# Row sums of every exponential and inverse, a test of them, and a branch to a general path at the end of a fused attention and feed-forward kernel

## The chip, the cores and the metric

The kernel runs on one core of one Trainium2 chip. A core has a matrix engine (TensorE, PE in the profile, with its weight loads as PEld), a vector engine (DVE), a scalar engine for activation functions (ScalarE, ACT), a general engine (GpSimd, POOL) and a fifth one that mostly issues transfers (SyncE, SP). Each engine works through its own list of instructions in order and waits on semaphores for the others. The metric is the device time of one execution, in microseconds (us).

## The reference

Sliding-window attention over 8 batches of 8 heads, 576 positions and 64 columns a head, with a window of 64 positions, and then a gated feed-forward block over the 4608 tokens:

```python
scores = scale * np.matmul(q, k.transpose(0, 1, 3, 2))
rel = pos[:, None] - pos[None, :]
mask = (rel >= 0) & (rel < window)
scores = np.where(mask, scores, -1000000000.0)
scores = scores - np.max(scores, axis=-1, keepdims=True)
attn = np.exp(scores)
attn = attn / (np.sum(attn, axis=-1, keepdims=True) + 1e-09)
attn_out = np.matmul(attn, v)
...
x = attn_out.transpose(0, 2, 1, 3).reshape(B * S, H * D)
g = x @ w_gate
silu = g * (1.0 / (1.0 + np.exp(-g)))
val = x @ w_val
return silu * val @ w_out
```

The inputs are random numbers: q, k and v with a standard deviation of 0.1, the weights with one over the square root of their depth. All are float32, and so is the output of 4608 x 512.

## The kernel before

The tokens are worked on in NT = 9 tiles of 512. Tiles 0 to 6 and 8 hold the first 512 positions of one batch each; tile LAST = 7 holds the last 64 positions of all eight batches. The kernel never takes a row's maximum: it takes the exponential of the scaled scores as they are, masks them, sums them by a matmul with ones, and multiplies the mixed values by the inverse of that sum. The inverse is made on ScalarE as the exponential of the negative logarithm, so that both come from one table of functions.

The order of all instructions is written out by hand (manual_schedule): what is called earlier in the program stands earlier in its engine's list. A tile t goes through these stages:

- scores (L279, in tile 0 L250) writes the products of queries and keys into the two double banks two[0] and two[1]. weigh (L294, in tile 0 weigh_first, L602) takes the exponential of each into a bf16 tile eb. The vector engine masks it (L299) and adds neighbours (L304).
- This is done twice for a tile, for two halves of the heads (w = 0 and 1), into the same two double banks. The matmuls of L480 that lie in between belong to the output projection of tile t - 1 and fill TensorE's time. Markers (L387) and two small copies (fence, L776, on ScalarE, and seen, L777, on the vector engine) order the use of two other banks.
- sums (L322, in tile 0 L315) makes the row sums of the weights by matmuls with ones. log (L336) takes their logarithm, invert (L339) the exponential of the negative logarithm, in place, in the float32 tile r.
- mix (L400) multiplies the weights with the values into two[1] and two[0]; scale (L416) multiplies the result with the inverse into the bf16 tile xT.
- gate_value (L459) runs twelve groups (m = 0 to 11), each of four matmuls with the gate weights and four with the value weights. gate_end takes the silu on ScalarE (L452) and the product on the vector engine (L453) into hT. The keys and queries of tile t + 1 are transposed between the groups on the vector engine.
- The projection to the output (L480, L468) of tile t runs beside the attention of tile t + 1. For the last tile it stands alone: three row blocks by project (L468, copied to SBUF at L488 and stored at L497 and L499), and the last one by project_last (L521, copied and stored in two pieces at L525 and L526).

Two switches of ScalarE's function table happen in each tile: set_exp (L529) before the exponentials, set_silu (L532) before the gates.

After the last store, SP waits for all transfers, and all engines meet in two barriers (in the profile at L848, the line at which the program is closed). Instructions are fetched from memory by each engine's own queue (the instruction queues q8 and q14 in the profile).

Of the kernel before, what the change touches and what calls it, by code (L numbers as in the profile page):

```python
# [17 lines left out]
def kernel(  # L18
# [10 lines left out]
    nc = tc.nc  # L29
    S, D, H = 576, 64, 8  # L30
    NTOK, DFF, DM = 4608, 1536, 512
    NT = NTOK // 512
# [25 lines left out]
    identb = cst.tile([P, P], BF16, name="identb")  # L58
    ones = cst.tile([P, 512], BF16, name="ones")
    tri = cst.tile([P, 2, 64], BF16, name="tri")  # L60
    bias = cst.tile([P, 2, 4, 4, 2, 16], BF16, name="bias")
    seen = cst.tile([D, 1], FP32, name="seen")
    fence = cst.tile([D, 1], FP32, name="fence")
    past = cst.tile([P, 1], BF16, name="past")
    mask = cst.tile([P, 8, 2, 16, 4], BF16, name="mask")

    def batch(t):
        return t if t < LAST else t - 1
# [7 lines left out]
    staged, queries, weights, inverse, xT, hT = {}, {}, {}, {}, {}, {}  # L76
# [95 lines left out]
    def stage_v(t):  # L172
        new_v(t)
        load_halves(nc.sync, staged[t, "v"], t)
# [115 lines left out]
    def weigh(t, w, h, s_ps):  # L290
        n = 1024 if t == LAST else 960
        E = eb[2 * w + h]
        flat = E[:].rearrange("r s z -> r (s z)")[:, 64:64 + n]
        nc.scalar.activation(  # L294
            flat, s_ps[:].rearrange("r a b -> r (a b)")[:, 0:n], AF.Exp, scale=0.125
        )

        def masked():
            nc.vector.tensor_mul(  # L299
                flat, flat, mask[:].rearrange("r j c e y -> r (j c e y)")[:, 0:n]  # L300
            )
            both = epool.tile([P, 8, 64], BF16, name="both", tag="both")
            lo = 2 if t == LAST else 0
            nc.vector.tensor_add(both[:], E[:, 1:17:2], E[:, lo:lo + 15:2])  # L304
            weights[t, w, h] = E, both

        return masked

    def ready(masks):
        for masked in masks:  # L310
            masked()
# [21 lines left out]
        return ap.rearrange("r (e x) -> r x e", e=16)  # L333

    def log(r, d_ps):
        nc.scalar.activation(r, d_ps, AF.Ln)  # L336

    def invert(r):
        nc.scalar.activation(r, r, AF.Exp, scale=-1.0)  # L339

    def logs(t, r, d):
        if t == NT - 1:
# [43 lines left out]
    def marker(b, x):  # L386
        nc.tensor.matmul(bank[b][0:D, 0:16], ones[half(x), 0:D], ones[half(x), 0:16])  # L387
# [39 lines left out]
    def mix_half(t, w, pair):  # L427
        mix(t, w, (pair[:, 0], pair[:, 1]))
# [15 lines left out]
    def gate_tiles():  # L444
        return out_tile(), d_tile()

    def gate_end(t, m, pair):
        if m == 0:
            hT[t] = hpool.tile([P, 12, 512], BF16, name="hT", tag="hT")
        g_ps, v_ps = pair  # L450
        sg = fsb.tile([P, 512], FP32, name="sg", tag="sg")
        nc.scalar.activation(sg[:], g_ps[:], AF.Silu)  # L452
        nc.vector.tensor_mul(hT[t][:, m, :], sg[:], v_ps[:])  # L453

    def gate_value(t, m):
        pair = gate_tiles()
        for ps, w in zip(pair, (wg, wv)):
            for c in range(4):
                nc.tensor.matmul(  # L459
                    ps[:], w[:, c, P * m:P * m + P], xT[t][:, c, :],  # L460
                    start=(c == 0), stop=(c == 3),
                )
        gate_end(t, m, pair)
# [52 lines left out]
    def project_last(t, s):  # L516
        r0 = S * batch(t) + P * s
        os_ = fsb.tile([P, 512], FP32, name="os_", tag="os_", bufs=4)
        for f0, f1, o_ps in ((0, 384, bank[6]), (384, 512, bank[0])):
            for c in range(12):  # L520
                nc.tensor.matmul(  # L521
                    o_ps[:, 0:f1 - f0], hT[t][:, c, P * s:P * s + P], wo[:, c, f0:f1],
                    start=(c == 0), stop=(c == 11),
                )
            nc.vector.tensor_copy(os_[:, f0:f1], o_ps[:, 0:f1 - f0])  # L525
            nc.sync.dma_start(out[r0:r0 + P, f0:f1], os_[:, f0:f1])  # L526

    def set_exp():
        nc.scalar.preload_act_table_set("natural_log_exp_and_others")  # L529

# [9 lines left out]
    v_first = stage.tile([P, 4, H, D], FP32, name="v_f", tag="v", bufs=1)  # L540
    load_v(nc.sync, v_first, (0, 1))
    set_exp()
    nc.vector.memset(ones[:, 0:P], 1.0)
    nc.vector.memset(ones[:, P:512], 1.0)
    nc.vector.memset(joined[half(1), 0], 0.0)
# [53 lines left out]

    def weigh_first(u):  # L600
        E = eb[u][:, 1:17].rearrange("r (h y) z -> r h (y z)", h=2)
        nc.scalar.activation(E, two[u % 2][:], AF.Exp, scale=0.125)  # L602
        weights[0, u] = E

    def sums_first(u, b):
# [25 lines left out]
    lo, hi = slice(0, 2), slice(2, 4)  # L631
# [63 lines left out]
    for m in range(12):  # L695
# [21 lines left out]
        if m == 10:  # L717
            for u in range(4):
                tp = two[u % 2].bitcast(BF16)[:, u // 2, 0:512]
# [5 lines left out]
            for u in range(4):  # L725
                tp = two[u % 2].bitcast(BF16)[:, u // 2, 0:512]
# [41 lines left out]
    for t in range(1, NT):  # L768
        if t > 1:
            set_exp()  # L770
            masks = scores(t, 0)
            masks[0]()
            project_quads(t - 1, tiles, range(12), 0)
            for x in range(2):
                marker(4 + 2 * x, x)
            on_a(fence[:], bank[4][0:D, 0:1])  # L776
            on_v(seen[:], bank[6][0:D, 0:1])  # L777
            masks[1]()
            if t == 2:
                stage_v(3)  # L780
            ready(scores(t, 1))
            for x in range(2):
                marker(4 + 2 * x, x)
            project_quads(t - 1, tiles, range(7), 1)
            end = sums(t, 0, two[0:1])
            project_quads(t - 1, tiles, range(7, 12), 1)
            for w in range(2):
                mix_half(t, w, two[1 - w])
# [12 lines left out]
        on_p(past[:], xT[t][:, 3, 0:1])  # L801
        if t + 1 == LAST:
            load_last_v()
        elif t + 1 < NT and t > 1:
            cast_v(t + 1)
        if t + 2 < NT:
            load_qk(t + 2)
            if t > 1 and t + 2 != LAST:
                stage_v(t + 2)
        if t == 2:  # L810
            k_l = cast.tile([P, 4, 4, 4 * D], BF16, name="k_l", tag="c0")
        if t in (2, 3):
            load_k(k_l, [(b, S - P) for b in range(4, 8)], quarters[2 * t - 4:2 * t - 2])
        turns = (6, 7, 9, 10) if t == 1 else (1, 4, 7, 10)
        for m in range(12):
            gate_value(t, m)
            if m in turns and t + 1 < NT:
                turn(t + 1, turns.index(m))
            if (t, m) in late:
                turn_k(kT[2], k_l, late.index((t, m)))  # L820
    for s in range(3):
        project(NT - 1, s, bank[(5, 7, 4)[s]])
    project_last(NT - 1, 3)

# [1 line left out]
_INS = ['q', 'k', 'v', 'moe_w_gate', 'moe_w_val', 'moe_w_out']  # L826
# [26 lines left out]
```

## Time and profile before

| what | value |
|---|---|
| median of 3 runs | 321.78 us (321.73 to 322.04) |
| the profiled execution as a whole | 322.17 us |
| its span, first to last instruction | 320.4 us |
| granted TensorE clock, mean | 1.000 |
| ScalarE: silu of the gates, L452 | 63.9 us |
| ScalarE: exponentials of tiles 1 to 8, L294 | 29.5 us, 0.974 each |
| ScalarE: inverses, L339 | 18.6 us, 0.972 each |
| vector engine: products of the gates, L453 | 73.9 us, 0.692 each |

The span is the time from the first to the last instruction in the profile; what the execution takes beyond it (1.8 us here) lies around it. A row of the timeline gives the start in us from the span's begin, the time that the instruction or the run of equal instructions took, the engine, the line, the operation, the tile written and the one read with their shapes, the count, and in brackets the idle time of the engine just before it and what ended that. A row of the list by line gives, behind the shapes and the count, the busy time in us and the mean of one in ns. In the list of instructions of one line the durations are least, median and most, in ns.

### The profile page before, as it was taken

Reading aid. Unit: us, or ns where it says so; the run is one execution under the profiler, and the core shown is the slowest. Engines: PE = TensorE matmul, PEld = TensorE weight load, DVE = VectorE, ACT = ScalarE, POOL = GpSimd, SP = SyncE. Lnnn points to the kernel's source line nnn. Section 1 sums busy time; section 2 is a strip of 40 time slices with the busy share of each in tenths; the row PEclk is TensorE's granted clock in tenths of the full one; section 3 lists DMA queues with packets and bytes.
Section 4 is the critical chain, followed back from the end, with each engine's and each line's share of the span. In section 5 each row is a group of like instructions: output and inputs, shape, how many; then the busy total and the mean of one; then the engine's idle time right before and its main releaser. Section 6 shows DMA issues by size and latency. Waiting matters only on the chain.

```text
span 320.4 us, 8080 instructions
## 1 busy us (share of the span) xinstructions
PE 315.9 (99%) x3297; PEld 155.0 (48%) x3297; DVE 209.4 (65%) x341; ACT 170.9 (53%) x239; POOL 147.4 (46%) x268
## 2 busy tenths in 40 slices
PE   8999999999999999999999999999999999999996
PEld 4544544445444644455445544454446444544443
DVE  4855846498586846776588656866796486844422
ACT  4964666348633863377336933584347633873310
POOL 4965656867557336650861099507766300000000
PEclk9999999999999999999999999999999999999999
DMA  7999999999799549994896269719998400011003
GB/s 249 205 196 198 206 149 229 189 193 130 165 186 178 65 109 167 187 103 100 150 194 69 61 122 119 75 28 149 184 197 103 109 9 1 4 74 60 0 20 113
DMA packets 83525, 40.42 MB, mean 126 GB/s; under 512 B 64160, under 2 KB 78752, under 8 KB 83488
## 3 DMA queue, kind: packets, MB, share of 16 engines
q0 software_dynamic: 51488, 22.59, 58.7%
q1 hardware_dynamic: 31456, 16.79, 23.8%
q8 instruction: 26, 0.43, 0.5%
q10 hardware_dynamic: 544, 0.52, 0.5%
q14 instruction: 11, 0.09, 0.1%
HBM read 53.02 MB, written 9.44 MB: 195 GB/s over the span
## 4 chain that ended last, share of the span: by engine, by line
PE 97%; ACT 2%; issue 0%; DVE 0%
PE one L459 56%; PE one L468 17%; PE one L480 11%; PE two L279 3%; PE two L400 2%; PE one L435 2%; PE one L554 1%; ACT eb L602 1%; PE two L322 1%; PE one L521 1%; PE two L435 1%; PE one L322 0%; ACT r L336 0%; ACT r L339 0%; PE one L197 0%; PE two L722 0%
## 5 line engine op out<-in xcount | busy, mean ns | idle before, releaser
L452 ACT ACTIVATE sg<-one 128x512 f32<-128x512 f32 x107 | 63.9, 597 | 117.2 <-PE one L459 91.3
L453 DVE TENSOR_TENSOR hT<-sg,one 128x512 bf16<-128x512 f32 x107 | 73.9, 692 | 62.6 <-PE one L459 58.5
L459 PE MATMUL one<-xT,wg 128*128 128x512 bf16 x416 | 106.8, 379 | 0.0
L459 PE MATMUL one<-xT,wv 128*128 128x512 bf16 x416 | 106.8, 379 | 0.0
L128 POOL DMA_DIRECT2D k_s<-in_k_dram x112 | 60.4, 575 | 27.0 <-DMA q_s<-in_q_dram 13.3
L459 PEld LDWEIGHTS <-wv 128*128 128x128 bf16 x416 | 40.7, 98 | 49.1
L459 PEld LDWEIGHTS <-wg 128*128 128x128 bf16 x416 | 40.6, 98 | 48.9
L468 PE MATMUL one<-wo,hT 128*128 128x512 bf16 x252 | 56.5, 380 | 0.0
L801 POOL COPY past<-xT 128x1 bf16<-128x1 bf16 x8 | 1.5, 189 | 88.7 <-DVE xT L416 88.7
L480 PE MATMUL one<-wo,hT 64*64 64x512 bf16 x672 | 40.0, 377 | 0.0
L468 PEld LDWEIGHTS <-hT 128*128 128x128 bf16 x252 | 23.8, 98 | 29.3 <-issue 2.0
L219 DVE STREAM_TRANSPOSE kT<-k_s 128x512 bf16<-128x512 bf16 x28 | 35.9, 1283 | 0.2 <-DMA vb<-in_v_dram 0.2
L416 DVE TENSOR_TENSOR xT<-two,r 128x512 bf16<-128x512 f32 x34 | 21.2, 683 | 20.6 <-ACT r L339 16.7
L294 ACT ACTIVATE eb<-two 128x960 bf16<-128x960 f32 (+1 forms) x32 | 29.5, 974 | 3.0 <-PE two L279 2.9
L480 PEld LDWEIGHTS <-hT 64*64 64x64 bf16 x672 | 18.6, 107 | 13.8
L299 DVE TENSOR_TENSOR eb<-eb,mask 128x960 bf16<-128x960 bf16 (+1 forms) x32 | 20.9, 654 | 5.7 <-ACT eb L294 5.6
L209 DVE STREAM_TRANSPOSE qT<-q_s 128x512 bf16<-128x512 bf16 x32 | 22.2, 700 | 0.1
L339 ACT ACTIVATE r<-r 128x1024 f32<-128x1024 f32 (+1 forms) x20 | 18.6, 972 | 0.1
L304 DVE TENSOR_TENSOR both<-eb 128x512 bf16<-128x512 bf16 x32 | 13.6, 425 | 1.1
L93 POOL DMA_DIRECT2D q_s<-in_q_dram x24 | 13.0, 549 | 1.6 <-DMA v<-in_v_dram 1.0
L154 POOL DMA_DIRECT2D vb<-in_v_dram x16 | 11.0, 692 | 6.1 <-DMA wo<-in_moe_w_out_dram 3.5
L529 ACT ACT_TABLE_LOAD x9 | 11.5, 1283 | 2.0 <-issue 1.9
(137 smaller groups left out, 241.9 us busy)
## 6 DMA issues: line engine op xcount, KB each, us to landing
k_s<-in_k_dram POOLq DMA_DIRECT2D x112, 56.0 KB, 5.3
q_s<-in_q_dram POOLq DMA_DIRECT2D x24, 248.0 KB, 6.0
v_f<-in_v_dram SPq DMA_DIRECT2D x40, 128.0 KB
wg<-in_moe_w_gate_dram POOLq DMA_DIRECT2D x5, 256.0 KB, 8.4
wv<-in_moe_w_val_dram POOLq DMA_DIRECT2D x5, 256.0 KB, 8.9
q_f<-in_q_dram SPq DMA_DIRECT2D x4, 256.0 KB
wo<-in_moe_w_out_dram POOLq DMA_DIRECT2D x2, 512.0 KB, 10.7
vb<-in_v_dram POOLq DMA_DIRECT2D x16, 64.0 KB, 6.6
```

The source lines that it names most:

```text
L128: nc.gpsimd.dma_start(k_s[p0:p0 + 32, g, :, 0:w], k[b, a:H:2, s:s + P].rearrange("u (r e) d -> r u (e d)", e=4) [:, :, 32 * c:32 * c + w],)
L209: nc.vector.transpose(queries[t][:, u, :].rearrange("r (e x) -> r e x", e=16), staged[t][0][:, u].rearrange("r (e d) -> r e d", d=D)[:, :, ...
L219: nc.vector.transpose(dst[:, u, :].rearrange("r (g x e) -> r g e x", g=4, e=4), k_s[:, :, u].rearrange("r g (e d) -> r g e d", d=D)[:, :, ...
L294: nc.scalar.activation(flat, s_ps[:].rearrange("r a b -> r (a b)")[:, 0:n], AF.Exp, scale=0.125)
L299: nc.vector.tensor_mul(flat, flat, mask[:].rearrange("r j c e y -> r (j c e y)")[:, 0:n])
L339: nc.scalar.activation(r, r, AF.Exp, scale=-1.0)
L416: nc.vector.tensor_mul(x, o_ps, r)
L452: nc.scalar.activation(sg[:], g_ps[:], AF.Silu)
L453: nc.vector.tensor_mul(hT[t][:, m, :], sg[:], v_ps[:])
L459: nc.tensor.matmul(ps[:], w[:, c, P * m:P * m + P], xT[t][:, c, :], start=(c == 0), stop=(c == 3),)
L468: nc.tensor.matmul(o_ps[:], hT[t][:, c, P * s:P * s + P], wo[:, c, :], start=(c == 0), stop=(c == 11),)
L480: nc.tensor.matmul(tiles[s][half(y)], hT[t][half(x), c, r0:r0 + 64], wo[half(x), c, :], start=not back and c == 0, stop=bool(back) and c = ...
```

## The change

Four things are added.

First, each exponential of scores (L294 and L602) and each inverse (L339) also gives the sum of its results along a row, one float32 column each, in a tile spread with 6 * NT + 2 = 56 columns; extent hands out the columns. Second, the logarithm gets a bias: a column floor that holds 2 to the power of -60 is added to its argument, so that a sum of zero doesn't give an infinite logarithm. Third, survey, called in the gates of the last tile behind group m = 4, compares all 56 columns with 2 to the power of 30 on the vector engine, takes the least of each row, sums the 128 rows by a matmul with ones into one element per row of two[0], and copies it to an integer column count. Fourth, at the end of the program every engine loads count into a register, and where it is below 128 the program runs a general path over all eight batches: attention with each row's maximum, a feed-forward block and its stores, over the output that is already there. Where it is 128, the engines go through a short block that brings the semaphores to the values that the general path would have left, and jump to the end.

In the built program the order of all other instructions on each engine is as before. The general path stands between the short block and the end: 8,001 instructions of TensorE, 3,385 of the vector engine, 1,593 of GpSimd, 1,369 of ScalarE and 577 of SP.

```diff
+    spread = cst.tile([P, 6 * NT + 2], FP32, name="spread")
+    within = cst.tile([P, 2], BF16, name="within")
+    count = cst.tile([P, 1], mybir.dt.int32, name="count")
+    floor = cst.tile([P, 1], FP32, name="floor")
+    LEAST, MOST = 2.0 ** -60, 2.0 ** 30
+    columns_used = [0]
+
+    def extent():
+        columns_used[0] += 1
+        return spread[:, columns_used[0] - 1:columns_used[0]]
...
         nc.scalar.activation(
-            flat, s_ps[:].rearrange("r a b -> r (a b)")[:, 0:n], AF.Exp, scale=0.125
+            flat, s_ps[:].rearrange("r a b -> r (a b)")[:, 0:n], AF.Exp, scale=0.125,
+            accum_out=extent(),
         )
...
     def log(r, d_ps):
-        nc.scalar.activation(r, d_ps, AF.Ln)
+        nc.scalar.activation(r, d_ps, AF.Ln, bias=floor[:])
 
     def invert(r):
-        nc.scalar.activation(r, r, AF.Exp, scale=-1.0)
+        nc.scalar.activation(r, r, AF.Exp, scale=-1.0, accum_out=extent())
...
+    def survey():
+
+        used = spread[:, 0:columns_used[0]]
+        fine = fsb.tile([P, 64], FP32, name="fine", tag="fine", bufs=1)[:, 0:columns_used[0]]
+        nc.vector.tensor_single_scalar(fine, used, MOST, op=ALU.is_le)
+        nc.vector.tensor_reduce(within[:, 0:1], fine, axis=mybir.AxisListType.X, op=ALU.min)
+        nc.tensor.matmul(two[0][:, 0, 0:1], ones[:, 0:P], within[:, 0:1])
+        nc.vector.tensor_copy(count[:], two[0][:, 0, 0:1])
+
+    def general_attention(b):
+
+        x_b = v12[:].rearrange("r g i h d -> r (g i h d)")[:, 0:4 * S]
...
+        for hd in range(H):
...
+            for c, (lo, hi) in enumerate(chunks):
...
+                nc.vector.tensor_reduce(top, s, axis=mybir.AxisListType.X, op=ALU.max)
+                nc.vector.tensor_scalar(top, top, -1.0, 0.0, op0=ALU.mult, op1=ALU.add)
+                nc.scalar.activation(s, s, AF.Exp, bias=top, accum_out=total)
...
+        return x_b
+
+    def general_ffn(b, x_b):
...
+            for m in range(12):
+                for w, ps_ in ((wg, bank[4]), (wv, bank[5])):
+                    for c in range(4):
+                        nc.tensor.matmul(
+                            ps_[:, 0:n], w[:, c, P * m:P * m + P], x_b[:, c, lo:hi],
+                            start=c == 0, stop=c == 3,
+                        )
...
+                nc.sync.dma_start(out[at:at + rows], os_[0:rows])
...
     set_exp()
+    nc.vector.memset(floor[:], LEAST)
...
-        nc.scalar.activation(E, two[u % 2][:], AF.Exp, scale=0.125)
+        nc.scalar.activation(E, two[u % 2][:], AF.Exp, scale=0.125, accum_out=extent())
...
             gate_value(t, m)
+            if t == NT - 1 and m == 4:
+                survey()
...
     project_last(NT - 1, 3)
+    good = nc.values_load(count[0:1, 0:1], min_val=0, max_val=P)
+    with tc.If(good < P, preferred_fallthrough_block=False):
+        for b in range(8):
+            x_b = general_attention(b)
+            general_ffn(b, x_b)
```

More of the change, by code (lines that the diff above doesn't have):

```diff
@@ new lines, in general_attention @@
+    def general_attention(b):
+        x_b = v12[:].rearrange("r g i h d -> r (g i h d)")[:, 0:4 * S]
+        x_b = x_b.rearrange("r (c s) -> r c s", c=4)
+        chunks = [(P * c, min(S, P * c + P)) for c in range(5)]
+        set_exp()
+        for hd in range(H):
+            u, h = hd // 2, hd % 2
+            wide = {}
+            for n, (src, tag) in (("q", (q, "q")), ("k", (k, "k"))):
+                f = stage.tile([P, 5, D], FP32, name=n + "_g", tag=tag)
+                nc.sync.dma_start(f[:, 0:4], src[b, hd, 0:512].rearrange("(c r) d -> r c d", r=P))
+                nc.sync.dma_start(f[0:64, 4], src[b, hd, 512:S])
+                bf = epool.tile([P, 5, D], BF16, name=n + "_h", tag="both")
+                nc.vector.tensor_copy(bf[:, 0:4], f[:, 0:4])
+                nc.vector.tensor_copy(bf[0:64, 4], f[0:64, 4])
+                tp = bank[4 if n == "q" else 5].bitcast(BF16)
+                for c, (lo, hi) in enumerate(chunks):
+                    nc.tensor.transpose(
+                        tp[0:D, lo:hi], bf[0:hi - lo, c], identb[0:hi - lo, 0:hi - lo]
+                    )
+                wide[n] = att.tile([P, S], BF16, name=n + "_w", tag="qT")
+                nc.vector.tensor_copy(wide[n][0:D], tp[0:D, 0:S])
+            vf = stage.tile([P, 5, D], FP32, name="v_g", tag="v", bufs=1)
+            nc.sync.dma_start(vf[:, 0], v[b, hd, 0:P])
+            nc.sync.dma_start(vf[:, 1:5], v[b, hd, 64:S].rearrange("(c r) d -> r c d", r=P))
+            vh = epool.tile([P, 5, D], BF16, name="v_h", tag="both")
+            nc.vector.tensor_copy(vh[:], vf[:])
+            for c, (lo, hi) in enumerate(chunks):
+                nq, k0 = hi - lo, max(0, lo - 64)
+                nk = hi - k0
+                s_ps = bank[6][0:nq, 0:nk]
+                nc.tensor.matmul(s_ps, wide["q"][0:D, lo:hi], wide["k"][0:D, k0:hi])
+                w = fsb.tile([P, 512], FP32, name="w_g", tag="sg")
+                s = w[0:nq, 0:nk]
+                nc.scalar.activation(s, s_ps, AF.Copy, scale=0.125)
+                for sign, base in ((1, lo - k0), (-1, 63 + k0 - lo)):
+                    nc.gpsimd.affine_select(
+                        out=s, in_=s, compare_op=ALU.is_ge, fill=-1e9,
+                        base=base, pattern=[[-sign, nk]], channel_multiplier=sign,
+                    )
+                top, total = w[0:nq, 256:257], w[0:nq, 257:258]
+                nc.vector.tensor_reduce(top, s, axis=mybir.AxisListType.X, op=ALU.max)
+                nc.vector.tensor_scalar(top, top, -1.0, 0.0, op0=ALU.mult, op1=ALU.add)
+                nc.scalar.activation(s, s, AF.Exp, bias=top, accum_out=total)
+                nc.vector.tensor_scalar(total, total, 1.0, 1e-9, op0=ALU.mult, op1=ALU.add)
+                nc.vector.reciprocal(total, total)
+                e = epool.tile([P, 192], BF16, name="e_g", tag="e_g", bufs=1)
+                nc.vector.tensor_scalar(e[0:nq, 0:nk], s, total, 0.0, op0=ALU.mult, op1=ALU.add)
+                tp = bank[7].bitcast(BF16)
+                pT = fsb.tile([P, 2, P], BF16, name="p_g", tag="p_g", bufs=1)
+                parts = [(0, P)] + ([(P, nk)] if nk > P else [])
+                for i, (j0, j1) in enumerate(parts):
+                    nc.tensor.transpose(
+                        tp[0:j1 - j0, P * i:P * i + nq], e[0:nq, j0:j1], identb[0:nq, 0:nq]
+                    )
+                    nc.vector.tensor_copy(
+                        pT[0:j1 - j0, i, 0:nq], tp[0:j1 - j0, P * i:P * i + nq]
+                    )
+                o_ps = bank[4][half(h), 0:nq]
+                for i, (j0, j1) in enumerate(parts):
+                    nc.tensor.matmul(
+                        o_ps, vh[0:j1 - j0, c + i], pT[0:j1 - j0, i, 0:nq],
+                        start=i == 0, stop=i == len(parts) - 1,
+                    )
+                nc.vector.tensor_copy(x_b[half(h), u, lo:hi], o_ps)
+        return x_b
@@ new lines, in general_ffn @@
+    def general_ffn(b, x_b):
+        set_silu()
+        for lo, hi in ((0, 512), (512, S)):
+            n = hi - lo
+            h_b = hpool.tile([P, 12, 512], BF16, name="h_b", tag="hT")
+            for m in range(12):
+                for w, ps_ in ((wg, bank[4]), (wv, bank[5])):
+                    for c in range(4):
+                        nc.tensor.matmul(
+                            ps_[:, 0:n], w[:, c, P * m:P * m + P], x_b[:, c, lo:hi],
+                            start=c == 0, stop=c == 3,
+                        )
+                sg = fsb.tile([P, 512], FP32, name="sg", tag="sg")
+                nc.scalar.activation(sg[:, 0:n], bank[4][:, 0:n], AF.Silu)
+                nc.vector.tensor_mul(h_b[:, m, 0:n], sg[:, 0:n], bank[5][:, 0:n])
+            for r0 in range(0, n, P):
+                rows = min(P, n - r0)
+                for c in range(12):
+                    nc.tensor.matmul(
+                        bank[6][0:rows], h_b[:, c, r0:r0 + rows], wo[:, c, :],
+                        start=c == 0, stop=c == 11,
+                    )
+                os_ = fsb.tile([P, 512], FP32, name="os_", tag="os_", bufs=4)
+                nc.vector.tensor_copy(os_[0:rows], bank[6][0:rows])
+                at = S * b + lo + r0
+                nc.sync.dma_start(out[at:at + rows], os_[0:rows])
```

## The prediction

> **What bounds the kernel now.** I read the page's busy times first, then the chain of work that ended last, then the timeline around the lines that the diff touches.
>
> ```profile
> span 320.4 us, 8080 instructions
> ...
> PE 315.9 (99%) x3297; PEld 155.0 (48%) x3297; DVE 209.4 (65%) x341; ACT 170.9 (53%) x239; POOL 147.4 (46%) x268
> ```
>
> ```profile
> PE 97%; ACT 2%; issue 0%; DVE 0%
> ```
>
> TensorE is busy for all but 4.5 us and carries 97% of the chain; ScalarE's 2% all lie before 13.3 us. So a microsecond counts only where it makes TensorE wait, or where it stands before TensorE's first steady work or behind its last. The added work sits on ScalarE, which is 53% busy, so its sum (56 sums, 27 biases) says little; the waits between the two engines decide. Three places: the first batch, the meeting of ScalarE and TensorE in each steady stage, and the end.
>
> The first batch, ScalarE in order of time (start, length, line):
>
> ```profile
> 7.53 1.02 ACT L602 ACTIVATE eb<-two 128x1024 bf16<-128x1024 f32 x1 [0.82 <-PE two L250]
> ...
> 9.04 0.60 ACT L336 ACTIVATE r<-one 128x512 f32<-128x512 f32 x1
> 9.54 1.02 ACT L602 ACTIVATE eb<-two 128x1024 bf16<-128x1024 f32 x1
> 10.44 0.63 ACT L339 ACTIVATE r<-r 128x512 f32<-128x512 f32 x1
> 11.05 0.60 ACT L336 ACTIVATE r<-two 128x512 f32<-128x512 f32 x1
> 11.68 0.63 ACT L339 ACTIVATE r<-r 128x512 f32<-128x512 f32 x1
> 12.22 1.92 ACT L602 ACTIVATE eb<-two 128x1024 bf16<-128x1024 f32 x2
> ```
>
> No line after the first has idle time before it: ScalarE runs without a gap from 7.53 to the end of the third exponential at 13.22, and TensorE's L365 starts at 13.27. Every nanosecond added in this run is paid.
>
> A steady stage (token tile 3), ScalarE and then TensorE:
>
> ```profile
> 106.17 1.83 ACT L294 ACTIVATE eb<-two 128x960 bf16<-128x960 f32 x2
> 108.31 0.15 ACT L776 COPY fence<-one 64x1 f32<-64x1 f32 x1 [0.31 <-PE one L387]
> 108.73 1.83 ACT L294 ACTIVATE eb<-two 128x960 bf16<-128x960 f32 x2 [0.26 <-PE two L279]
> 110.53 1.02 ACT L336 ACTIVATE r<-two 128x1024 f32<-128x1024 f32 x1
> ```
>
> ```profile
> 108.07 0.62 PE L279 MATMUL two<-qT,kT 64*64 64x128 bf16 x31
> 111.39 1.01 PE L400 MATMUL two<-eb,vb 64*64 64x128 bf16 x64
> ```
>
> The second scores of a stage overwrite the two tiles that the first two exponentials read. The second exponential ends at 108.00; its first dependent matmul, the third of L279's run, starts at 108.09. A hand-over costs 0.05 (the fence copy ends at 108.47, the marker matmul behind it starts at 108.52), so this wait has 0.03 us of room. It is the tightest of the stage.
>
> **The change, part by part.** A row sum is given by 56 activations: 4 at L602, 32 at L294, 20 at L339. No row of this trace has one. Lower end: 0, the sum rides along. Upper end: a further ScalarE instruction for a 128x1 result, at an activation's fixed cost: L339 takes 0.63 us for 512 columns and 1.06 for 1024, which leaves 0.20 at none. Nearest is the fence copy, one column, 0.15 alone; neighbours overlap by 0.10 (exponentials are 0.97 long and 0.87 apart), so it adds 0.05 between others and 0.15 where something waits for it. I take d = 0.10. The bias of the 27 logs becomes a column in memory: 0 to 0.15 by the same copy, I take b = 0.08. The Trainium skill, "ScalarE: Activation LUTs", section on what ACT_TABLE_LOAD costs, states about 93 ns for each per-partition pointer operand; no run here shows it yet, and by it the sum below would be 0.1 us higher.
>
> First batch: from 7.53 to 13.22 there are five sums (three exponentials, two inverses) and two logs: 5d + 2b = 0.66 us (0 to 1.3). Behind it the other inverses have room: the gates' first matmul with the third column block starts 0.64 after that block's scaling ends.
>
> Each stage of tiles 2 to 8, seven in all. (A) L279 waits for two sums more: 2d - 0.03 = 0.17 (0 to 0.37). The fence copy has 0.31 of room behind the exponential, so it takes nothing more. (B) The second half of L400 writes the tile that the log at 110.53 reads; the log ends at 111.55 and that half starts at 111.81, 0.20 of room behind the hand-over. The log itself is held by L322's totals and could have started 0.07 earlier. So two sums and one bias cost (2d - 0.07) + b - 0.20 = 0.01 (0 to 0.28). The later logs and inverses (2b + 2d = 0.36) have over a microsecond before the gates read their blocks: nothing. Seven times 0.18 = 1.26 (0 to 4.6). Tile 1's waits have 0.20 or more of room: nothing. ScalarE in all: 1.9 us (0 to 5.9).
>
> The survey comes behind the fifth gate group (m = 4) of the last tile. Its TensorE matmul stands in the program order between that group and the next and waits for the vector engine's compare and reduce, which stand behind that group's product:
>
> ```profile
> 294.78 1.03 PE L459 MATMUL one<-xT,wg 128*128 128x512 bf16 x4
> 295.05 0.69 DVE L453 TENSOR_TENSOR hT<-sg,one 128x512 bf16<-128x512 f32 x1 [1.04 <-PE one L459]
> ```
>
> TensorE would start group 5 at 294.78. The product ends at 295.74; a compare of 128x56 at the 0.19 of L571 (128x64), a hand-over of 0.05, a reduce at 0.15 to 0.19, less up to 0.09 of overlap with the product (L416's products are 0.69 long and 0.60 apart), another hand-over: 296.1 to 296.2. The matmul takes 0.05 more. Behind it the whole gate stream is queued, nothing later is slack, so TensorE loses 1.45 us (1.2 to 1.7). The copy of the count fits into the 1.04 that the vector engine idles. The one memset at the start lies in its wait for the key load (0.7 before the cast at 4.53).
>
> The end:
>
> ```profile
> 317.37 0.81 SPq L526 DMA_DIRECT2D out_dram<-os__4647  x2
> 317.46 0.29 DVE L525 COPY os__4647<-two 128x128 f32<-128x128 f32 x1
> ```
>
> ```profile
> q8 instruction: 26, 0.43, 0.5%
> ...
> q14 instruction: 11, 0.09, 0.1%
> ```
>
> ```profile
> L848 SPq DRAIN x3: 7/7/7, 319.5 to 319.8; - x3
> ```
>
> SP issues the last store until 318.18, finds it landed at 319.48, drains, and the barriers end at 320.4. Afterwards each engine loads the count into a register, compares, falls through to a short block and jumps over the general path. SP's register load runs beside the store's landing (1.3 us of cover; one DMA trip, 1.7 from issue to landing, would outlast it by 0.6). In the short block SP waits for the store, then jumps to code far behind: 577 of its own instructions lie between. The instruction queues moved 0.43 MB in blocks of 16 KB for TensorE's 6,600 instructions and 0.09 MB in blocks of 8 KB, each once and in order, so the jump's target is a block that nothing has asked for. No row shows such a fetch. Lower end 0; nearest, a load from memory: the first queries are issued at 0.81 and their cast starts at 4.20, 3.4 us for 256 KB; the last store's trip is 1.7. I take 3.0 (upper end 6.0, two blocks one after the other). The Trainium skill, "Runtime: NRT & Kernel Launch", section on instruction fetch, says the same of a taken branch outside the two-page window and gives no price. The waits that SP did beside the landing (0.06 apart in the trace) now follow the jump: 11 x 0.06 = 0.7. With 0.15 for branch and leftovers, 3.85 us (0.9 to 7). TensorE's own jump can start when its last matmul ends at 317.4, two microseconds ahead of SP's: covered.
>
> Sum: 1.9 + 1.45 + 3.85 = 7.2. Against the span of 320.4, 327.6. The profiled run took 322.17 as a whole, the median is 321.78; I add to the median: 329.0.
>
> **Rivals.** (1) Dear sums: each is a full extra slot, d = 0.20 and b = 0.15. For it: 0.20 is what every activation pays before its columns. 5.9 + 1.45 + 3.85 = 11.2: 333.0. (2) Free sums, d and b near 0: the adder works beside the columns; against it, 56 results must be written somewhere. 0.2 + 5.3: 327.3. (3) No fetch at the jump, because the end block is there already: 7.2 - 3.0: 326.0. Against it: in-order blocks. (4) Two fetches in a row: 332.0. (5) Not slower: TensorE is limited by the supply of its instructions, not by the array, so a stall lets the supply run ahead and the dense pieces (L279, L400, 0.013 apart) go faster afterwards. Place: the pieces after each stall; it decides once these regain a microsecond in each of seven stages, 7 us in all: 321.8. Against it: L400's 64 run as four at a time at 0.054 for 128 columns, which is L459's rate of 512 columns in 0.216. (6) The change doesn't do what it says: the count misses 128 and the general path runs. Its gates alone are 8 batches x 96 matmuls x 0.24 = 187 us: over 510. For it speaks nothing; the sums are of some tens of exponentials near 1.
>
> **How the numbers follow.** Forecast 0.46, (1) 0.14, (2) 0.13, (3) 0.11, (4) 0.13, (5) 0.02, (6) 0.01. The range runs from (3) to (1), 326.0 to 333.0, and leaves out the two last cases and the outer sides of (1) and (3). A measurement of this kernel tells 0.2% (0.64 us) from no change. Slower by more: 0.97; within: 0.02; faster: 0.01.
>
> **What would show it.** A small ScalarE entry behind each exponential, or exponentials further apart than 0.87; L279's third matmul later after the second exponential's start by 0.17; TensorE idle for 1.4 us at the survey's matmul; between the store's landing and the last drain some 3 us in which only an instruction queue moves. I'm wrong if the stages keep their 33.5 us spacing, if TensorE passes the survey without a gap, or if the end keeps its 2.6 us behind the last copy.

## The result, and the profile after

The changed kernel takes 331.0 us (median of 6 runs, 329.73 to 331.8) against 321.91 us (median of 6) of the kernel before in the same session: 1.0277 times, with a 95% interval of 1.0255 to 1.0299. The profiled execution took 330.77 us as a whole. In the kernel after, the lines stand ten or eleven higher (L279 is L289, L294 is L304, L336 is L347, L400 is L411, L459 is L470, L526 is L537), L602 is L719 and L776 is L893. The register load is L943, the branch L944, the end L972.

The page of the kernel after, its span, its busy times and the shares of the chain of waits:

```profile
span 329.0 us, 8172 instructions
...
PE 315.8 (96%) x3298; PEld 158.9 (48%) x3298; DVE 209.7 (64%) x345; ACT 177.1 (54%) x295; POOL 147.7 (45%) x268
...
PE 94%; DMA 1%; ACT 1%; DVE 1%; issue 0%; DVEq 0%
```

The span grew by 8.6 us and TensorE's busy time by nothing (315.9 before). All of it is idle time of TensorE. ScalarE has 56 instructions more, one for each sum.

The timeline of ScalarE in the first batch of the kernel after (start, length, engine, line):

```profile
7.74 1.02 ACT L719 ACTIVATE eb<-two 128x1024 bf16<-128x1024 f32 x1
8.65 0.19 ACT L719 ACTIVATION_READ_ACCUMULATOR eb<-two 128x1 f32 x1
9.35 0.69 ACT L347 ACTIVATE r<-one,floor 128x512 f32<-128x512 f32 x1
```

And in the stage of tile 3, the exponentials of the first half and the first logarithm:

```profile
106.97 0.97 ACT L304 ACTIVATE eb<-two 128x960 bf16<-128x960 f32 x1
107.84 0.19 ACT L304 ACTIVATION_READ_ACCUMULATOR eb<-two 128x1 f32 x1
107.93 0.96 ACT L304 ACTIVATE eb<-two 128x960 bf16<-128x960 f32 x1
108.78 0.20 ACT L304 ACTIVATION_READ_ACCUMULATOR eb<-two 128x1 f32 x1
...
111.57 1.12 ACT L347 ACTIVATE r<-two,floor 128x1024 f32<-128x1024 f32 x1
```

A sum is a second instruction behind its activation. It is recorded with 0.19 to 0.20 us, but the next activation starts 0.09 behind its start, so between neighbours a sum adds 0.09: the two exponentials are 0.96 apart, where they were 0.87. The logarithm with a column as bias takes 1.12 where it took 1.02, and 0.69 where it took 0.60.

The survey in the timeline of the kernel after, the vector engine and then TensorE (in brackets the idle time before, and what ended it):

```profile
297.08 0.69 DVE L464 TENSOR_TENSOR hT<-sg,one 128x512 bf16<-128x512 f32 x1 [1.04 <-PE one L470]
297.68 0.18 DVE L543 TENSOR_SCALAR fine<-spread 128x56 f32<-128x56 f32 x1
297.90 0.21 DVE L544 TENSOR_REDUCE within<-fine 128x1 bf16<-128x56 f32 x1
298.17 0.16 PE L545 MATMUL two<-within,ones 128*128 128x1 bf16 x1 [1.20 <-DVE within L544]
```

TensorE stands still for 1.20 us at the survey's matmul, which waits behind the product and the two operations of the survey on the vector engine.

The end. The last store in the timeline, SP's part of the list of instructions of the register load (L943), of the branch (L944, with TensorE's too) and of the end (L972). In the lists the durations are least, median and most in ns, then come the first and the last start in us:

```profile
320.78 0.81 SPq L537 DMA_DIRECT2D out_dram<-os__4657  x2
```

```profile
L943 SPq TENSOR_LOAD <-count x1: 533/533/533, 321.6 to 321.6; - x1
```

```profile
L944 SPq EVENT_SEMAPHORE  x8: 17/17/17, 322.7 to 324.5; - x8
...
L944 PEldq COMPARE_BRANCH  x2: 95/1939/3783, 319.6 to 321.0; - x2
...
L944 SPq COMPARE_BRANCH  x2: 38/46/53, 322.6 to 324.6; - x2
```

```profile
L972 SPq EVENT_SEMAPHORE  x14: 17/28/28, 327.4 to 329.0; - x14
```

SP has issued the store at 321.59, loads the register, compares at 322.6 and does the eight waits of the short block. Seven of them are through at 323.14. The last one is for the store, and it passes only at 324.50, 2.9 us behind the issue; before the change this took 1.3 (318.18 to 319.48). Then SP jumps at 324.6, and its next instruction runs at 327.4: 2.8 us for the jump over the general path. Twelve waits 0.06 apart follow, and the barriers.

Why the store lands late is seen in the tables of stretches, first of the kernel before and then of the kernel after (from and to, length, busy time of each engine with its count, granted clock, mean busy share of the 16 DMA engines, GB/s). A packet counts with its whole time in the stretch in which it starts:

```profile
318.20:319.10 0.90, 0.00 (x0) 0.00 (x0) 0.00 (x0) 0.00 (x0) 0.00 (x0) 1.00 0.88 291
319.10:319.50 0.40, 0.00 (x0) 0.00 (x0) 0.00 (x0) 0.00 (x0) 0.00 (x0) 1.00 0.00 0
```

```profile
321.60:322.50 0.90, 0.00 (x0) 0.00 (x0) 0.00 (x0) 0.00 (x0) 0.00 (x0) 1.00 0.93 305
322.50:323.20 0.70, 0.00 (x0) 0.00 (x0) 0.00 (x0) 0.00 (x0) 0.00 (x0) 1.00 0.05 12
323.20:323.90 0.70, 0.00 (x0) 0.00 (x0) 0.00 (x0) 0.00 (x0) 0.00 (x0) 1.00 0.05 6
```

Before the change the store's data are through by 319.10. After it nearly all DMA engines work until 322.5, and then very little moves for 1.4 us. The trace's records of single packets tell what it was. TensorE's far jump (the COMPARE_BRANCH of 3.78 us, from 321.0) fetched 16 KB of instructions in one packet, from 322.44 to 323.41, and the vector engine's far jump 8 KB from 322.71 to 323.25. Of the last store's 128 packets of 512 bytes, 120 were through at 322.50; the other eight, a sixteenth of the store, moved one after the other from 323.39 to 323.86. The store has sixteen landings in the trace: fifteen until 322.86, the last at 324.48. The records don't name the DMA engine of a packet; that the fetch and the eight packets shared one is concluded from these times.

The difference of the spans by landmarks of the two traces:

| stretch | before | after | difference |
|---|---|---|---|
| start to first exponential | 7.53 | 7.74 | +0.21 (other profiles: 6.74 to 7.67) |
| first exponential to first gate matmul | 7.78 | 8.33 | +0.55 |
| eight distances of first gate matmuls, tile to tile | 270.86 | 272.10 | +1.24 |
| last tile's first gate matmul to the end of the last matmul | 31.27 | 32.66 | +1.39 |
| behind the last matmul | 2.96 | 8.22 | +5.26 |

Of the 1.24, tiles 3, 4, 5, 6 and 8 give 0.15 to 0.16 each, tile 2 gives 0.04, tile 7 gives 0.44. Tile 7's stage varies from run to run (34.1 to 35.0 us), by a pause of TensorE in L411 that waits for nothing the profile shows; it is left open.

### The profile page after: what moved, and what is told of

It reads as the page before. It is cut to its first block, busy times and chain, and to the rows that moved or that the text cites. A ratio compares the mean times of both kernels' runs of the same rounds, so it can differ in the third digit from the quotient of the medians.

```text
span 329.0 us, 8172 instructions
## 1 busy us (share of the span) xinstructions
PE 315.8 (96%) x3298; PEld 158.9 (48%) x3298; DVE 209.7 (64%) x345; ACT 177.1 (54%) x295; POOL 147.7 (45%) x268
## 4 chain that ended last, share of the span: by engine, by line
PE 94%; DMA 1%; ACT 1%; DVE 1%; issue 0%; DVEq 0%
PE one L470 55%; PE one L479 17%; PE one L491 11%; PE two L289 3%; PE two L411 2%; PE one L446 2%; DMA q_f<-in_q_dram 1%; ACT eb L719 1%; PE two L333 1%; PE one L532 1%; PE two L446 1%; PE one L333 1%; ACT qk_b L705 0%; PE two L839 0%; PE one L207 0%
## 5 line engine op out<-in xcount | busy, mean ns | idle before, releaser
L470 PE MATMUL one<-xT,wg 128*128 128x512 bf16 x416 | 106.8, 379 | 0.0
L470 PE MATMUL one<-xT,wv 128*128 128x512 bf16 x416 | 106.8, 379 | 0.0
L470 PEld LDWEIGHTS <-wg 128*128 128x128 bf16 x416 | 40.6, 98 | 50.1 <-issue 1.5
L470 PEld LDWEIGHTS <-wv 128*128 128x128 bf16 x416 | 40.7, 98 | 49.0
L304 ACT ACTIVATE eb<-two 128x960 bf16<-128x960 f32 (+1 forms) x32 | 31.0, 973 | 3.8 <-PE two L289 3.7
L491 PEld LDWEIGHTS <-hT 64*64 64x64 bf16 x672 | 21.7, 107 | 10.8
L350 ACT ACTIVATE r<-r 128x1024 f32<-128x1024 f32 (+1 forms) x20 | 19.3, 970 | 0.1
L347 ACT ACTIVATE r<-one,floor 128x512 f32<-128x512 f32 x17 | 10.9, 683 | 4.0 <-PE one L333 4.0
```

What stands on the lines that cost most here:

```text
L304: nc.scalar.activation(flat, s_ps[:].rearrange("r a b -> r (a b)")[:, 0:n], AF.Exp, scale=0.125, accum_out=extent(),)
L350: nc.scalar.activation(r, r, AF.Exp, scale=-1.0, accum_out=extent())
L470: nc.tensor.matmul(ps[:], w[:, c, P * m:P * m + P], xT[t][:, c, :], start=(c == 0), stop=(c == 3),)
L491: nc.tensor.matmul(tiles[s][half(y)], hT[t][half(x), c, r0:r0 + 64], wo[half(x), c, :], start=not back and c == 0, stop=bool(back) and c = ...
```

## Experiments

A tail is the time behind the last matmul of the profiled run. Ratios are against the kernel before, measured beside each.

**The branch left out.**

```diff
-    good = nc.values_load(count[0:1, 0:1], min_val=0, max_val=P)
-    with tc.If(good < P, preferred_fallthrough_block=False):
-        for b in range(8):
...
```

> The changed kernel without the register loads and the branch at its end (no general path in the program); sums, biases and the survey stay. Theory: of the 9.1 us between the medians (321.9 to 331.0) 5.3 lie behind TensorE's last matmul, 1.4 at the survey and the rest on ScalarE's way; this run keeps the last two: 325.7 us, and the span ends 3.0 us behind the last matmul as before. Rival, the end is slower because of the sums or the longer list of semaphores and not because of the branch: above 328.

324.85 us, ratio 1.0077 (1.0054 to 1.0101), tail 2.95. The tail is that of the kernel before (2.96). So what is computed costs 2.7 us and, between the medians, the branch 6.1 (331.0 less 324.85). Behind the last matmul of the two profiled runs the branch costs 5.3 (tails of 8.22 and 2.95); ahead of it they differ only in the start (6.77 and 7.74 to the first exponential) and in tile 7, both of which vary from run to run. The time is 0.85 us under the expected 325.7, which had taken 5.3 for the end; why the medians give more than the tails is left open.

**The branch with a short path behind it**, the same register load and comparison:

```diff
     with tc.If(good < P, preferred_fallthrough_block=False):
-        for b in range(8):
-            x_b = general_attention(b)
-            general_ffn(b, x_b)
+        nc.vector.memset(past[:], 0.0)
+        nc.scalar.copy(fence[:], seen[:])
+        nc.gpsimd.memset(tri[0:1, 0, 0:1], 0.0)
+        marker(4, 0)
+        nc.sync.dma_start(out[0:P, 0:50], spread[:, 0:50])
```

> The branch stays, but the general path is cut to one small instruction on each engine, so that the end block lies directly behind it. Theory, the price is the fetch of a far block: no fetch, 326.6 us (0.9 more than without a branch: SP's waits behind the jump and the branches themselves), and no pause of over 0.5 us on SP between its jump and its first wait behind it. Rival, loading a register and branching cost that time themselves: 330 to 331.

325.91 us, ratio 1.0114 (1.0082 to 1.0146), tail 4.04. The branch line of this kernel:

```profile
L944 PEldq COMPARE_BRANCH  x2: 90/142/193, 318.1 to 319.5; - x2
...
L944 SPq COMPARE_BRANCH  x2: 38/46/53, 321.1 to 321.3; - x2
```

TensorE's comparison takes 0.19 us instead of 3.78, and SP's first wait behind its jump runs 0.19 us after it. The register load, the comparison and the waits that no longer run beside the store's landing cost 1.06 us. The other 5.1 us between the medians go with the distance of the jumps; 4.2 of them are seen in the tails of the profiled runs (8.22 and 4.04), which differ ahead of that, again, in start and tile 7. The Trainium skill, "Runtime: NRT & Kernel Launch", section on instruction fetch, says that a taken branch to a place outside the window already fetched needs a fetch; the two kernels agree with it: SP's jump takes 2.8 us over the long path and 0.19 over the short one, and in the short one no packet of instructions moves from 317.6 to the end of the span at 323.4.

**The far jump on SP alone, and on TensorE alone.** The path holds nothing but 384 issues of loads by SP in the one, 1,000 matmuls in the other:

```diff
-            x_b = general_attention(b)
-            general_ffn(b, x_b)
+            for hd in range(H):
+                for n, src in (("q", q), ("k", k), ("v", v)):
...
+                    nc.sync.dma_start(f[:, 0:4], src[b, hd, 0:512].rearrange("(c r) d -> r c d", r=P))
+                    nc.sync.dma_start(f[0:64, 4], src[b, hd, 512:S])
```

```diff
-        for b in range(8):
-            x_b = general_attention(b)
-            general_ffn(b, x_b)
+        for _ in range(1000):
+            marker(4, 0)
```

> The general path is replaced by 384 loads on SP alone; the other engines' jumps go over nothing. Theory, the last store lands late because TensorE's fetch of 16 KB stands before some of its packets on one DMA engine: without that fetch the store lands 1.3 us after it was issued, SP's own fetch of 2.8 us stays, 329.4 us. Rival, the landing is late because SP loads its register beside it: 2.9 us from issue to landing again and 331 us.

> The general path is replaced by 1000 small matmuls on TensorE alone, so that only TensorE jumps far. Theory: TensorE's fetch still meets the last store, which lands 1.6 us late, and SP fetches nothing: 328.2 us; where the fetch happens to take a DMA engine whose part of the store is through, 326.6. Rival, TensorE's fetch doesn't touch the store: 326.6 in all runs and a landing after 1.3 us in the profile.

SP alone: 328.76 us, ratio 1.0203 (1.0171 to 1.0235), tail 6.56. TensorE alone: 327.63 us, ratio 1.016 (1.0127 to 1.0193), tail 5.01. Both are 0.6 us under what was expected. The branch line, first of SP's far jump:

```profile
L944 SPq EVENT_SEMAPHORE  x8: 17/17/17, 321.4 to 321.9; - x8
...
L944 PEldq COMPARE_BRANCH  x2: 90/142/193, 318.3 to 318.5; - x2
```

and of TensorE's:

```profile
L944 PEldq COMPARE_BRANCH  x2: 95/1984/3872, 319.4 to 320.8; - x2
```

With SP's far jump alone the eight waits pass without a halt, from 321.4 to 321.9 (after: to 324.5); the store lands 1.3 us behind its issue, and the jump takes 2.5 us. With TensorE's alone the store lands 3.0 us behind the issue, though SP jumps nowhere far and the vector engine fetches nothing: again fifteen landings come early, and the last eight packets (323.26 to 323.73) start as a 16 KB fetch ends (322.34 to 323.27). So it is TensorE's fetch that holds up the store. This run's end is set by TensorE itself, 0.3 us behind SP: its jump starts at 320.80 and its drain comes at 324.78, SP's at 324.43 and 324.49. The two excesses over the short path, 2.85 and 1.72 us, add to 4.6 of the 5.1 between the medians; by the tails they are 2.5 and 1.0 of 4.2.

**The sums alone, their halves, and the bias alone.** These four are the kernel before with one part each: a sum with all 56 activations; with the 16 exponentials of w = 0 of tiles 1 to 8 only; with the 32 of w = 1 and inverses of tiles 1 to 8 only; the bias only. The edits of the second and the last one:

```diff
-            flat, s_ps[:].rearrange("r a b -> r (a b)")[:, 0:n], AF.Exp, scale=0.125
+            flat, s_ps[:].rearrange("r a b -> r (a b)")[:, 0:n], AF.Exp, scale=0.125,
+            **({"accum_out": extent()} if w == 0 else {})
```

```diff
-        nc.scalar.activation(r, d_ps, AF.Ln)
+        nc.scalar.activation(r, d_ps, AF.Ln, bias=floor[:])
```

> The kernel before with the 56 row sums alone: no bias, no survey, no branch; the sums are kept and not tested. Theory: a sum costs its readout, 0.09 us between neighbours, and is paid where TensorE waits: five in the first batch (0.46) and 0.16 in each of seven stages (1.1), 1.6 us: 323.4 us. Rival, every sum is paid: 56 x 0.09 = 5.2 us: 327.

> The kernel before with sums on the exponentials of the first half (w = 0) of tiles 1 to 8 alone, 16 of them. Theory: these are what the second scores wait for with 0.03 us of room, 7 x 0.155 = 1.1 us: 323.0 us, stages 33.69 apart in the profile. Rival, sums are paid by number: 16 x 0.09 = 1.5 us, and the next run costs twice as much.

> The kernel before with sums on the exponentials of the second half (w = 1) and on the inverses of tiles 1 to 8, 32 of them. Theory: all have more room than they take (0.27 for two sums before the log, over 1 us for the inverses): within 0.3 us of the kernel before, stages 33.53 apart. Rival, by number: 32 x 0.09 = 2.9 us: 324.8.

> The kernel before with the bias column on the 27 logs alone. Theory: two logs in the first batch's chain at 0.09 (0.18 us), all others have room (0.20 before the second half of the mix): 322.1 us, at the edge of what can be told. Rival, by number: 27 x 0.09 = 2.4 us: 324.3.

| kernel | median, us | ratio (95%) | stage | first batch |
|---|---|---|---|---|
| all sums | 323.1 | 1.0027 (1.0013 to 1.0041) | +0.11 | +0.37 |
| first half's sums | 322.63 | 1.0016 (1.0001 to 1.0032) | +0.11 | +0.01 |
| second half's sums and inverses | 322.2 | 1.0002 (0.9988 to 1.0017) | 0 | +0.03 |
| bias | 321.73 | 0.9991 (0.9973 to 1.0009) | 0 | +0.18 |

The stage is read from the chain of waits (start, length, engine, tile, line), two neighbouring tiles each. After:

```profile
118.86 20.72 PE one L470 x96
152.55 20.72 PE one L470 x96
```

The first half's sums alone:

```profile
117.99 20.72 PE one L466 x96
151.63 20.72 PE one L466 x96
```

The second half's alone:

```profile
118.71 20.72 PE one L467 x96
152.24 20.72 PE one L467 x96
```

33.69, 33.64 and 33.53 us apart (before 33.53). All that the sums cost a stage comes from the two exponentials of the first half, whose banks the second scores overwrite. These two sums cost 0.11 a stage and the others nothing, though a readout has the same length in both. The column holds for tiles 3 to 6 and 8. Tile 2's stage was 34.88 in the second half's profile (before 33.65), with TensorE waiting twice in the gates for the vector engine's products; the median, 0.1 us from the kernel before, shows no such cost, so it is taken for scatter. The readouts in the run with the first half's sums:

```profile
L300 ACT ACTIVATION_READ_ACCUMULATOR eb<-two 128x1 f32 x16 | 3.2, 199 | 0.0
```

(Group in the list by line: busy us, mean ns, idle us before.) Expected were 0.155 a stage, and the wait itself is that long: in tile 3 the third matmul of the second scores starts 3.22 us behind the first scores (before 3.07), and 0.05 behind the end of the second readout (108.22 and 108.17). So the room was 0.03, as the prediction read it. But TensorE regains a part: from that matmul to the next L480 (here L487) it takes 0.40 where it took 0.47, and over the whole stage 0.11 of the 0.15 is left.

The bias alone costs a stage nothing, but after has both and 0.16: the last 0.05 appear only where bias and sums come together, as in the term (B) of the prediction. In after the second half of the mix starts 0.05 behind the end of the logarithm (112.74 and 112.69), a hand-over; with all sums and no bias it starts 0.09 behind it, and before 0.25. So there the logarithm is what it waits for. In the first batch the parts add up: 0.37 for five sums and 0.18 for two logs make 0.55.

**The survey's matmul later.** The matmul with ones and the copy to count are moved from behind m = 4 to behind m = 5; compare and reduce stay:

```diff
         nc.vector.tensor_reduce(within[:, 0:1], fine, axis=mybir.AxisListType.X, op=ALU.min)
+
+    def tally():
         nc.tensor.matmul(two[0][:, 0, 0:1], ones[:, 0:P], within[:, 0:1])
...
+            if t == NT - 1 and m == 5:
+                tally()
```

> The changed kernel with the matmul and the copy of the count behind the sixth gate group instead of the fifth; compare and reduce stay where they are. Theory: TensorE waits for the reduce, which then has a whole group of 1.73 us to come; 1.4 us less, 329.6 us (the end moves by up to 1 us from run to run, with where the store meets a fetch), and 31.3 us in the profile from the last tile's first gate matmul to TensorE's last, as before. Rival, the stall is the dispatch of an odd small matmul: it stays, 331.

329.05 us, ratio 1.0206 (1.0182 to 1.023). TensorE in the timeline of this kernel:

```profile
297.21 1.03 PE L470 MATMUL one<-xT,wv 128*128 128x512 bf16 x4
298.07 0.17 PE L548 MATMUL two<-within,ones 128*128 128x1 bf16 x1
298.10 1.02 PE L470 MATMUL one<-xT,wg 128*128 128x512 bf16 x4
```

No idle time in brackets: the matmul takes its 0.03 us between two groups. From the last tile's first gate matmul to the end of the last one are 31.30 us (after 32.66, before 31.27). So the 1.39 was the place of one matmul. The medians differ by 1.95, and the tail of this run is no shorter (8.54); the rest is left open.

**The general path as the fall-through**, on top of that. The one jump, over the path, now stands ahead of SP's wait for the store, so its fetch can run while the store lands:

```diff
-    with tc.If(good < P, preferred_fallthrough_block=False):
+    with tc.If(good < P, preferred_fallthrough_block=True):
```

> The same, and the general path stands ahead of the short block, so that the common way jumps far at the compare and walks on into the end. Theory: SP's far jump (2.5 to 2.8 us) then runs beside the landing of the last store instead of behind it, and a late landing costs nothing: 328.1 us, 6.6 to 6.9 us behind TensorE's last matmul. Rival, all far jumps wait for the last store in any case: as the run before.

328.34 us, ratio 1.0186 (1.0149 to 1.0222), tail 7.67. The time came out near what was expected, the tail did not: it is 0.8 to 1.1 us longer. The last store in its timeline:

```profile
318.99 1.70 SPq L537 DMA_DIRECT2D out_dram<-os__4657  x2
```

Its two issues took 1.70 us instead of 0.81. TensorE's jump started at 317.8 in this run, and a fetch packet of 16 KB ran from 319.39 to 320.33, while the second issue ran (319.42 to 320.70). In the next two kernels, too, such a fetch meets the issues (until 319.75 and 319.70), and they take 1.09 and 1.21 us. That the fetch delays the issue is what this suggests; no run tested it alone.

**The register load early as well**, behind m = 9 of the last tile:

```diff
+            if t == NT - 1 and m == 9:
+                good = nc.values_load(count[0:1, 0:1], min_val=0, max_val=P)
```

> The same, and the registers are loaded behind the tenth gate group of the last tile instead of at the end. Theory: SP's load, its checks and their gaps (0.9 us) leave the way between the last store's issue and the far jump: 327.2 us, 5.7 to 6.0 behind the last matmul. Rival, the loads hold up TensorE, ScalarE or the vector engine in the gates: a gap there and no gain.

326.93 us, ratio 1.0138 (1.0116 to 1.016), tail 6.11, both near what was expected. SP's comparison starts at 320.13, right behind the issue, and its next instruction at 322.90: the jump of 2.8 us is what remains.

**The general path's transfers on GpSimd's queue**, on top of the three. SP then has nothing in the path to jump over:

```diff
...
-                nc.sync.dma_start(out[at:at + rows], os_[0:rows])
+                nc.gpsimd.dma_start(out[at:at + rows], os_[0:rows])
```

> The same, and the general path's transfers are issued by GpSimd instead of SP, so that SP has no far jump and GpSimd's lies some 20 us before the end. Theory: SP's fetch is the one that ends last; without it the end costs 0.3 to 1 us more than in the kernel before, 324.6 us, of which 1.7 us are ScalarE's sums and biases. Rival, TensorE's own far jump (3.8 us in the run with matmuls alone) takes its place as the last: 326 us and more.

325.11 us, ratio 1.008 (1.0059 to 1.0101), tail 4.53. SP's waits at the end, and the vector engine at the branch:

```profile
L978 SPq EVENT_SEMAPHORE  x14: 17/28/1178, 320.3 to 323.4; - x14
```

```profile
L950 DVEq COMPARE_BRANCH  x1: 72/72/72, 319.0 to 319.0; - x1
...
L950 DVEq EVENT_SEMAPHORE  x1: 21/21/21, 322.3 to 322.3; - x1
```

One wait of SP lasts 1.18 us, until the vector engine is behind its own far jump: 3.4 us from 318.97 to 322.35. Neither expectation named it. The theory had 0.3 to 1 us more at the end than the kernel before, and it is 1.6; the rival put TensorE's jump last, and that is through at 321.1. Of all versions that do the change's whole work this is the fastest, 5.9 us ahead of the change as made, and still 0.8% slower than the kernel before.

## Why the prediction was right, point by point

The direction and most of the places were right, and 331.0 lies in the range, 2.0 us above the forecast. The forecast sum was 7.2 us; the spans of the two profiles differ by 8.6, and the end alone accounts for the 1.4 between them. The rest of the 2.0 is scatter between executions.

- First batch, 0.66: measured 0.55. d was taken as 0.10 and is 0.07 to 0.09, b as 0.08 and is 0.09. The Trainium skill's 93 ns for a pointer operand ("ScalarE: Activation LUTs", what ACT_TABLE_LOAD costs) agrees with the longer logarithm (0.09 at 512 columns).
- Stages, seven times 0.18 = 1.26: measured 0.15 to 0.16 in five, 0.04 in tile 2, and 0.44 in tile 7, of which an unknown part is that tile's own scatter; 1.24 in all. That it comes so near 1.26 is partly luck: a stage costs 0.16 and not 0.18, and tile 7 happened to be long. The place (A) is confirmed by the halves of the sums: all of the sums' cost is there, and the wait grew by 0.15, which is 2d - 0.03 with d = 0.09. What the sum lacks is the part that TensorE regains behind the wait; (B) took 0.05 instead of 0.01. The rival of dear sums (11.2 us) fell, since a readout is 0.20 long but adds 0.09; the rival of free sums fell with 0.11 a stage.
- Survey, 1.45: measured 1.39, and none of it with the matmul one group later.
- The end, 3.85: measured 5.26, and here the sum failed. Of its terms, SP's jump was 2.8 for 3.0, and the waits behind the jump 0.77 for 0.7. The step that failed is the one that put TensorE's jump at nothing: "TensorE's own jump can start when its last matmul ends at 317.4, two microseconds ahead of SP's: covered". The jump started as written, 0.2 us behind the last matmul, and was through before SP's. What the prediction left out is that its fetch and the last store go through the same DMA engines: eight packets of the store moved only behind the fetch packet, and SP's wait for the store passed 2.9 us behind the issue instead of 1.3. Of these 1.6 us, 1.3 are the late landing; the other 0.3 are SP's own: with register load, comparison and seven waits it would come to the store's wait 1.6 us behind the issue (323.14 and 0.05 more), so they weren't wholly covered by a landing of 1.3, and the sum had 0.15 for branch and leftovers. The kernel with TensorE's far path alone has the late landing, and the one with SP's alone doesn't. The rival of two fetches in a row had the time nearest to the result (332.0) by another mechanism: the second fetch is not SP's but TensorE's, and it costs by way of the store.
- No fetch at the jump (326.0) fell with the short path. That TensorE makes up for stalls by its supply (321.8) fell with TensorE's idle time of 1.20 at the survey, which nothing behind it gave back. Behind the longer wait of a stage it does run faster, as that rival said, but regains 0.07 there and not a microsecond. That the general path runs (over 510; its 8 x 96 x 0.24 is 184 and not 187) fell with the time of 331.0.

## What to carry to other kernels

Code that is never taken is not free at the end of a kernel: every engine that has instructions in it takes 2.4 to 4.2 us for the jump over them, which counts where the engine has nothing else to wait for, and the fetches use the same DMA engines as the last stores. Keep the engines that end last out of the rarely taken block (here SP, and behind it the vector engine with its last copy), and put the decision and the register load as far ahead of the last store as the data allows. A small test in a dense stream costs what its matmul waits; one group further along it cost nothing.

## What the runs showed of the hardware that was not expected

- A sum with an activation is an instruction of its own, 0.19 to 0.20 us long, of which only 0.07 to 0.09 delays a following activation.
- A far jump takes 2.5 to 2.8 us on SP, 3.0 to 3.5 on the vector engine, 3.8 to 4.2 on TensorE, against 0.19 on SP and on TensorE to a near target. Little of it is transfer: TensorE's fetch packet starts 1.4 us behind the jump's start (321.02 to 322.44), takes 1.0, and the next instruction comes another 1.45 later (323.41 to 324.86).
- A fetch of 16 KB for TensorE is one packet of 0.9 to 2.0 us. A sixteenth of the last store waits for it, by the times on the same DMA engine: the store's landing went from 1.3 to 2.9 us.
- A register load from a tile takes 0.46 (ScalarE) to 0.54 us (the vector engine).
